# Retention woven into a two-layer network on one core: two of a block's four visits move to the first layer, and sums, casts and waits are placed anew

## The chip, the core and the metric

The kernel runs on 1 core of one Trainium2 chip. The metric is the device time of one launch in microseconds (us), the median of several runs. Before the change it is 301.63 us, with runs between 301.53 and 302.08.

Five engines work side by side, each through its own list of instructions in order: TensorE (PE; its weight loads are shown as PEld), VectorE (DVE), ScalarE (ACT), GpSimd (POOL) and SyncE (SP), which here only issues loads and DMA transposes. An engine waits for another by semaphores.

## The reference

Two parts, one after the other. The first is retention: for each of 8 batches and 8 heads, with 576 positions of 64 numbers, scores are multiplied by a decay that falls with the distance and is zero for later positions. The second is a network of two layers on the 4608 tokens.

```python
gamma = 1.0 - 2.0 ** (-5.0 - np.arange(H))
Dmat = np.where(rel >= 0, gamma[:, None, None] ** rel[None, :, :], 0.0)
attn = np.matmul(scale * np.matmul(q, k.transpose(0, 1, 3, 2)) * Dmat, v)
x = attn.transpose(0, 2, 1, 3).reshape(B * S, H * D)      # 4608 x 512
h = x @ w_in                                              # 4608 x 2048
out = (h * np.cos(h)) @ w_out                             # 4608 x 512
```

## The kernel before

The tokens are worked in nine blocks of 512 (`TB`, block number `j`). Blocks 0 and 1 have a warm-up order of their own; blocks 2 to 8 are one loop (lines 1056 to 1062).

**First layer of a block** (`mlp1`): sixteen groups `dt` of four matmuls 128x512, each into one of four accumulator banks `mm`. ScalarE makes the cosine (`cb`, line 552), VectorE multiplies (`gt`, line 554). Behind each group `steps1` may put a sum, a store, or nothing.

**Second layer** (`mlp2`): the product of 512 tokens x 2048 with 2048 x 512 is cut into halves of tokens, of the contraction and of the columns, and made from seven products of half size instead of eight (`product`, numbers 1 to 7). Each has sixteen matmuls 128x256. For this VectorE makes sums of halves of `gt` (`ssum`, kinds 1 to 4 in four pairs each, tile `ss`, line 576); sums of halves of `w_out` (`ts`) are made once. ScalarE keeps partial results (`keep`, tile `u`), VectorE adds them up (`total`, tile `osb`, line 642).

**Retention** runs in chunks `g` of 128 tokens, 36 in all. One "visit" (`visit`, `quarters`) holds up to 64 small matmuls 64x64 in one woven stretch on TensorE: the outputs of chunk g (in the accumulators `po` and `st`) and the scores and state of chunk g+1 (in `sc`). Behind it ScalarE copies the outputs into `xt`, the input of the first layer, VectorE masks the scores (`rt`, line 753) and adds the running state (`pf`, line 764), and ScalarE casts the state (`sm`, `sn`), the second of the two only at the next visit (`self.old`). Block j visits chunks 4j+4 to 4j+7, whose outputs block j+1 needs. All four visits stand in the second layer, between products: P1 P2 visit P5 visit P6 visit P7 visit P4 P3.

**A chunk's way in**: SP loads k, q and v (`load_g`), GpSimd casts k and scales q and v (`casts_g`, lines 357 to 365), SP transposes k and q by DMA (`turn_dma`, tile `kqt`). `prep(g)` emits the casts and the transposes of chunk g and then calls `pump`, which issues waiting loads of later chunks as long as at most `AHEAD` = 9 load buffers of 16 are taken (three for a chunk). So SP's list is transposes of one chunk, loads of a later one, and so on. In block j, `prep` takes chunks 4j+5 to 4j+8 behind groups 2, 5, 8 and 11. GpSimd is held by nothing but its data and the reuse of the nine slots of a chunk.

`group` makes one list of matmuls with one wait ahead of all of them: a product waits for every sum that it reads before its first matmul.

## Time and profile before

| what | value |
|---|---|
| median of the runs | 301.63 us (301.53 to 302.08) |
| the profiled execution's own time | 301.94 us |
| its span, first to last instruction | 300.2 us |
| mean granted TensorE clock | 0.994 |
| bytes moved by DMA | 49.70 MB |
| read from HBM, written to it | 36.70 MB, 9.44 MB |

The profile is one execution, on one core. "Busy" leaves out waits. In a list of instructions in order of time, a row has its start, the busy time of the merged run, engine, line, operation, tiles as out<-in, shapes and count; in brackets stands the idle time before it and what ended it. "issue" is idle time in which the engine waited for nothing that the profile shows. A window row gives for a stretch the busy time and the count of instructions of each engine, then the granted clock and the DMA's busy share (over 1 where packets of several queues overlap).

### The profile page before, as it was taken

What the parts mean: (1) busy time and instruction counts of PE and PEld (TensorE: products, weight loads), DVE (VectorE), ACT (ScalarE), POOL (GpSimd) and SP (SyncE); (2) the same over time, 40 slices, a digit from 0 to 9 for tenths busy, and PEclk for the clock granted to TensorE, in tenths of its full rate; (3) what the DMA queues carried; (4) which work ended last, traced back from release to release, by engine and by line L of the source; (5) the groups of instructions that cost most, each with busy time, mean ns of one, the idle gap of its engine ahead of it and who ended that gap; (6) DMA issues with size and microseconds to landing.
All of it is one profiled execution on the core that took longest, in us unless ns stands there. A gap on an engine that the chain in (4) does not pass through costs nothing.

```text
span 300.2 us, 8398 instructions
## 1 busy us (share of the span) xinstructions
PE 290.0 (97%) x3532; PEld 181.1 (60%) x3558; DVE 225.4 (75%) x465; ACT 180.7 (60%) x344; POOL 100.1 (33%) x120
## 2 busy tenths in 40 slices
PE   8999999999999999999999979999999999999996
PEld 3474455645454587458745755477547854885485
DVE  3666666766868976998699965979697869766973
ACT  6788435886457645774577435855585567465720
POOL 3670336663634654345436542525000000000000
PEclk9999999999999999999999989999999999999999
DMA  6999999999999999999999999999300130013013
GB/s 206 237 207 192 211 321 194 290 199 179 225 209 251 209 192 186 258 201 172 238 243 232 192 197 238 213 226 161 105 2 2 38 107 0 3 37 107 0 37 105
DMA packets 142325, 49.70 MB, mean 166 GB/s; under 512 B 125904, under 2 KB 141264, under 8 KB 142288
## 3 DMA queue, kind: packets, MB, share of 16 engines
q1 hardware_dynamic: 129280, 35.53, 66.7%
q10 hardware_dynamic: 8784, 9.44, 10.2%
q0 software_dynamic: 4224, 4.19, 8.5%
q8 instruction: 28, 0.46, 0.7%
q14 instruction: 9, 0.07, 0.1%
HBM read 36.70 MB, written 9.44 MB: 154 GB/s over the span
## 4 chain that ended last, share of the span: by engine, by line
PE 88%; DVE 8%; issue 2%; ACT 1%; DVEq 0%
PE mm L461 63%; PE mm L463 15%; DVE gt L554 3%; PE st L708 2%; DVE ss L576 2%; PE sc L708 2%; PE sc L461 2%; PE po L708 1%; PE po L461 1%; DVE rt L485 1%; PE st L461 1%; DVE pf L764 1%; DVE rt L753 0%; ACT cb L552 0%; ACT sb L342 0%
## 5 line engine op out<-in xcount | busy, mean ns | idle before, releaser
L552 ACT ACTIVATE cb<-mm,c_pih 128x512 bf16<-128x512 f32 (+3 forms) x156 | 100.7, 654 | 34.6 <-PE mm L463 34.4
L461 PE MATMUL mm<-xt,win 128*128 128x512 bf16 (+3 forms) x452 | 114.7, 362 | 0.8 <-DVE gt L554 0.3
L554 DVE TENSOR_TENSOR gt<-mm,cb 128x512 bf16<-128x512 f32 (+3 forms) x156 | 99.1, 646 | 20.9 <-ACT cb L552 17.9
L461 PEld LDWEIGHTS mm<-xt,win 128*128 128x128 bf16 x468 | 44.4, 98 | 47.4 <-DVE gt L554 1.3
L463 PE MATMUL mm<-xt,win 128*128 128x512 bf16 (+3 forms) x156 | 56.6, 363 | 0.4
L461 PE MATMUL mm<-wout,gt 128*128 128x256 bf16 (+1 forms) x298 | 49.2, 304 | 1.1 <-issue 0.8
L461 PE MATMUL mm<-ts,ss 128*128 128x256 bf16 x300 | 36.2, 273 | 1.1 <-DVE ss L576 1.0
L365 POOL TENSOR_TENSOR vb<-ld,wv 128x512 bf16<-128x512 f32 x27 | 29.6, 1095 | 22.8 <-DMA ld<-in_v_dram 13.8
L461 PEld LDWEIGHTS mm<-wout,gt 128*128 128x128 bf16 x306 | 28.2, 98 | 13.2 <-DVE gt L554 1.1
L342 POOL CAST kq<-ld 128x512 bf16<-128x512 f32 (+1 forms) x29 | 18.4, 634 | 49.8 <-DMA ld<-in_k_dram 47.9
L361 POOL TENSOR_TENSOR kq<-ld,uq 128x512 bf16<-128x512 f32 x27 | 28.9, 1071 | 14.6 <-DMA ld<-in_q_dram 14.4
L342 ACT ACTIVATE xt<-po 128x256 bf16<-128x256 f32 (+1 forms) x35 | 14.7, 419 | 27.4 <-PE st L708 18.8
L461 PEld LDWEIGHTS mm<-ts,ss 128*128 128x128 bf16 x300 | 27.8, 98 | 5.3 <-DVE ss L576 1.2
L753 DVE TENSOR_TENSOR rt<-sc,mh 128x256 bf16<-128x256 f32 x54 | 20.3, 417 | 12.9 <-PE st L708 9.7
L576 DVE TENSOR_TENSOR ss<-gt 128x512 bf16<-128x512 bf16 x56 | 26.9, 480 | 0.2
L642 DVE TENSOR_TENSOR osb<-mm,u 128x512 f32<-128x512 f32 x20 | 13.8, 688 | 17.3 <-PE mm L463 14.6
L463 PEld LDWEIGHTS mm<-xt,win 128*128 128x128 bf16 x156 | 15.2, 98 | 16.0
L342 ACT ACTIVATE u<-mm 128x512 f32<-128x512 f32 x21 | 12.5, 597 | 19.4 <-PE mm L463 19.3
L764 DVE TENSOR_TENSOR pf<-sc,pf 128x256 f32<-128x256 f32 x42 | 17.6, 420 | 2.0
L342 ACT ACTIVATE sm<-pf 128x256 bf16<-128x256 f32 x24 | 10.0, 417 | 10.6 <-DVE pf L764 8.7
L463 PE MATMUL mm<-wout,gt 128*128 128x512 bf16 (+1 forms) x46 | 15.9, 347 | 0.1
L461 PE MATMUL mm<-ts,gt 128*128 128x256 bf16 x105 | 13.9, 289 | 0.1
(154 smaller groups left out, 370.9 us busy)
## 6 DMA issues: line engine op xcount, KB each, us to landing
out_dram<-osb ACTq DMA_DIRECT2D x35, 256.0 KB, 4.3
ld<-in_k_dram SPq DMA_DIRECT2D x32, 256.0 KB, 4.9
ld<-in_q_dram SPq DMA_DIRECT2D x32, 256.0 KB, 4.8
ld<-in_v_dram SPq DMA_DIRECT2D x32, 256.0 KB, 6.2
win<-in_moe_w_in_dram POOLq DMA_DIRECT2D x4, 512.0 KB, 8.3
wout<-in_moe_w_out_dram POOLq DMA_DIRECT2D x4, 512.0 KB, 15.1
ld<-in_k_dram SPq DMA_DIRECT2D x8, 128.0 KB, 4.3
ld<-in_q_dram SPq DMA_DIRECT2D x8, 128.0 KB, 4.0
```

The lines of the kernel that those rows point to most:

```text
L342: fn = (lambda e: e.activation(o, x, AF.Copy)) if eng == "act" else (lambda e: e.tensor_copy(o, x))
L361: self.s.op("pool", lambda e: e.tensor_tensor(o, a, w, ALU.mult), reads=[bt, self.bUQ], writes=[self.bQB[i]])
L365: self.s.op("pool", lambda e: e.tensor_tensor(o2, a2, w2, ALU.mult), reads=[bt, self.bWV], writes=[self.bVB[i]])
L461: self.nc.tensor.matmul(o, a, b, **kw)
L463: return s.done("pe", self.nc.tensor.matmul(o, a, b, **kw), reads, writes)
L552: s.op("act", lambda e: e.activation(ci, mi, AF.Sin, bias=self.C_PIH.ap(), scale=1.0), reads=[bm, self.bC], writes=[self.bCB[i]])
L554: s.op("dve", lambda e: e.tensor_tensor(bass.AP(self.GT, dt * TB + o0, [[16 * TB, 128], [1, n]]), mi, ci, ALU.mult), reads=[bm, self.bCB[i ...
L576: self.s.op("dve", lambda e: e.tensor_tensor(self.s_(k, d), a, b, op), reads=rd, writes=[S[k - 1][p]])
L642: self.s.op("dve", lambda e: e.tensor_tensor(o, m, x, ALU.add), reads=[bm, self.bU[u]], writes=[self.bOSB[i]])
L708: inst = self.nc.tensor.matmul(o, a, c, **kw)
L753: s.op("dve", lambda e: e.tensor_tensor(bass.AP(self.RT[n % 2][x], 0, p3), bass.AP(self.SC[x], 0, p3), bass.AP(self.MH, 0, [[64, 128], [0, ...
L764: s.op("dve", lambda e: e.tensor_tensor(self.PF[t].ap(), u, self.PF[1 - t].ap(), ALU.add), reads=[self.bSU[t], self.bPF[1 - t]], writes=[s ...
```

## The change

- **Visits**: in block j the first two visits come in the first layer, behind groups 4 and 10; the third stands behind P2, the fourth behind P7. The order of the second layer is P1 P2 visit P6 P5 P7 visit P4 P3.
- **What follows a visit** (masks, copies into `xt`, adds, casts) is put on a list (`todo`) and emitted from it by `flush`: two entries behind each first-layer group, six or all at set places of the second layer, the rest ahead of the next visit.
- **Sums**: in the first layer only two pairs of kind 1 are left, behind group 14; all others stand in the second layer, in runs of four to six. (The last block has kind 3 in the first layer, behind groups 8 to 11.)
- **Products wait by pairs**: a product is four groups of four matmuls, each with a wait for its own pair of sums.
- **GpSimd** waits, behind group 0 of a first layer, for that group's last matmul (`need`), and `prep` takes chunks 4j+7 to 4j+10 behind groups 0, 3, 6 and 9; chunks 13 and 14 are taken during block 1's second layer.
- **Loads**: from chunk 16 on, up to 12 load buffers may be taken.

```diff
@@ product
-        self.group(mms, ra + rb, bms)
+        for p in range(4):
+            self.group([(bass.AP(ms[tt], tt * HN, [[512, 128], [1, HN]]), a(d, tt), b(d),
+                         dict(...)) for d in (2 * p, 2 * p + 1) for tt in tts],
+                       ra(p) + rb(p), bms)
@@ quarters
+        halves = [t for t in range(2) if n is not None and n % 9 != (4, 8)[t]]
+        for x in range(2):
+            self.todo += [(mask, x) if n is not None else None, (xt, x) if g is not None else None]
+        self.todo += [(add, t) if t in halves else None for t in range(2)] + [None, None]
+        for t in halves:
+            self.todo += [(cast, t), None]
+
+    def flush(self, n=None):
+        for _ in range(len(self.todo) if n is None else min(n, len(self.todo))):
+            u = self.todo.pop(0)
+            if u:
+                u[0](u[1])
@@ mlp2
         br = self.take()
         self.product(br, 2, True, True)
-        self.ssum(2, 0)
-        self.ssum(2, 1)
-        vis(0)
...
+        self.ssum(1, 2)
+        self.ssum(1, 3)
+        for p in range(4):
+            self.ssum(2, p)
+        for g in visits[:1]:
+            self.visit(g)
+        self.flush(6)
         self.product(bs, 6, False, False)
         self.keep(bs, 1)
+        self.flush()
+        i11 = self.total(br, 0)
+        if not last:
+            for p in range(4):
+                self.ssum(3, p)
+        bt = [(self.SC[t], self.bSC[t]) for t in range(2)] if last else self.take()
+        self.product(bt, 5, True, False)
         self.store(i11, j, 0, 0)
+        for p in range(4):
+            self.ssum(4, p)
         self.product(bs, 7, False, last)
         self.keep(bs, 2)
...
+        for g in visits[1:]:
+            self.visit(g)
+        self.flush(6)
@@ steps1
-        if dt in (2, 4, 6, 8):
-            self.ssum(3, dt // 2 - 1)
-        if dt in (10, 12, 14):
-            self.ssum(1, dt // 2 - 5)
+        if dt == 14:
+            self.ssum(1, 0)
+            self.ssum(1, 1)
+        if j == NTB - 1 and dt in (8, 9, 10, 11):
+            self.ssum(3, dt - 8)
@@ pump
-                if fn == self.load_g and sum(self.busy) + n > AHEAD:
+                if fn == self.load_g and sum(self.busy) + n > (AHEAD if a[0] < 4 * 4 else AHEAD + 3):
@@ emit
             if n in (1, 5, 9, 13):
                 self.visit(G0 + n // 4 - 1)
-            elif T and n:
+                self.flush()
+            if n in (6, 10):
+                self.prep(G0 + 3 + n // 5)
+            if T and n not in (0, 1, 5, 9, 13):
                 self.tsum("dve", *T.pop(0))
...
         for j in range(2, NTB):
+            g = 4 * j + 4 if j < NTB - 1 else NG
             for dt in range(16):
                 self.mlp1(j, dt)
+                self.flush(2)
                 self.steps1(j, dt)
-                if dt % 3 == 2 and dt < 12:
-                    self.prep(4 * j + 5 + dt // 3)
-            self.mlp2(j, range(4 * j + 4, 4 * j + 8) if j < NTB - 1 else [])
+                if dt == 0:
+                    self.s.need("pool", [self.last])
+                if dt % 3 == 0 and dt < 12:
+                    self.prep(g + 3 + dt // 3)
+                if dt in (4, 10) and g < NG:
+                    self.visit(g + dt // 6)
+            self.mlp2(j, range(g + 2, min(g + 4, NG)))
```

More of the change, by code (lines that the diff above doesn't have):

```diff
@@ L233, in __init__ @@
         self.order = [0, 1, 2, 3]
-        self.old = None
+        self.todo = []
     def build(self):
@@ L547, in mlp1 @@
                 dict(start=c == 0, stop=c == 3)) for c in range(4)]
-        self.group(mms, [self.bWIN[dt // 4]] + self.bXT[t0 // GR:(t0 + n) // GR], [bm])
+        self.last = self.group(mms, [self.bWIN[dt // 4]] + self.bXT[t0 // GR:(t0 + n) // GR], [bm])
         i = self.n_cb % self.NCB
@@ L602, in ga @@
             return (lambda d, tt: bass.AP(self.GT, (8 * kh + d) * TB + th * HT + 128 * tt, [[16 * TB, 128], [1, 128]]),
-                    self.bGT[8 * kh:8 * kh + 8])
+                    lambda p: self.bGT[8 * kh + 2 * p:8 * kh + 2 * p + 2])
         def sa(i):
             return (lambda d, tt: bass.AP(self.SS, ((i - 1) * 8 + d) * HT + 128 * tt, [[32 * HT, 128], [1, 128]]),
-                    self.bSS[i - 1])
+                    lambda p: [self.bSS[i - 1][p]])
         def wb(kh, nh):
             return (lambda d: bass.AP(self.WOUT, (8 * kh + d) * DM + nh * HN, [[16 * DM, 128], [1, HN]]),
-                    self.bWOUT[8 * kh:8 * kh + 8])
+                    lambda p: self.bWOUT[8 * kh + 2 * p:8 * kh + 2 * p + 2])
         def tb(i):
-            return (lambda d: bass.AP(self.TS, ((i - 1) * 8 + d) * HN, [[32 * HN, 128], [1, HN]]), [self.bTS[i - 1]])
+            return lambda d: bass.AP(self.TS, ((i - 1) * 8 + d) * HN, [[32 * HN, 128], [1, HN]]), lambda p: [self.bTS[i - 1]]
         (a, ra), (b, rb) = {1: (ga(0, 0), wb(0, 0)), 2: (ga(0, 1), wb(1, 0)), 3: (sa(4), wb(1, 1)),
                             4: (ga(1, 1), tb(4)), 5: (sa(1), tb(1)), 6: (sa(2), tb(2)), 7: (sa(3), tb(3))}[k]
-        mms = [(bass.AP(ms[tt], tt * HN, [[512, 128], [1, HN]]), a(d, tt), b(d),
-                dict(start=start and d == 0 and (tt == tts[0] or ms[0] is not ms[1]), stop=stop and d == 7, skip_group_check=True))
-               for d in range(8) for tt in tts]
-        self.group(mms, ra + rb, bms)
+        for p in range(4):
+            self.group([(bass.AP(ms[tt], tt * HN, [[512, 128], [1, HN]]), a(d, tt), b(d),
+                         dict(start=start and d == 0 and (tt == tts[0] or ms[0] is not ms[1]), stop=stop and d == 7,
+                              skip_group_check=True)) for d in (2 * p, 2 * p + 1) for tt in tts],
+                       ra(p) + rb(p), bms)
     def osb(self):
@@ L735, in quarters @@
                             [self.bQT[i]] + [self.bSM if t else self.bSN[(g - 1) % 2] for t in ts], [bXY[x]], None)]
-        if self.old:
-            sn, t, bsn = self.old
-            self.copy("act", sn.ap(), self.PF[t].ap(), [self.bPF[t]], [bsn])
-            self.old = None
-        self.weave(*[cross[x] + score[x] + state[x] + own[x] + past[x] for x in range(2)])
-        if g is not None:
-            x0 = CH * g % XR
-            w = self.bXT[x0 // GR:(x0 + CH) // GR]
-            for x in range(2):
-                t = self.copy("act", bass.AP(self.XT, 2 * x * XR + x0, [[NP * XR, 128], [XR, 2], [1, CH]]),
-                              bass.AP(self.XY[x], 0, [[512, 128], [CH, 2], [1, CH]]), [bXY[x]], [Buf()] if x else w)
-            for u in w:
-                u.w.append(t)
@@ L749, in quarters @@
-        if n is not None:
-            m = n % 9
-            for x in range(2):
-                p3 = [[512, 128], [64, NP], [1, 64]]
-                s.op("dve", lambda e: e.tensor_tensor(
-                    bass.AP(self.RT[n % 2][x], 0, p3), bass.AP(self.SC[x], 0, p3),
-                    bass.AP(self.MH, 0, [[64, 128], [0, NP], [1, 64]]), ALU.mult),
-                    reads=[self.bSC[x], self.bSU[x], self.bMH], writes=[self.bRT[n % 2][x]])
-            for t, sn, bsn in ((0, self.SM, self.bSM), (1, self.SN[n % 2], self.bSN[n % 2])):
-                if m == (4, 8)[t]:
-                    continue
-                u = bass.AP(self.SC[t], 256, [[512, 128], [1, NP * D_]])
-                if m == 4 * t:
-                    self.copy("dve", self.PF[t].ap(), u, [self.bSU[t]], [self.bPF[t]])
-                else:
-                    s.op("dve", lambda e: e.tensor_tensor(self.PF[t].ap(), u, self.PF[1 - t].ap(), ALU.add),
-                         reads=[self.bSU[t], self.bPF[1 - t]], writes=[self.bPF[t]])
-                if t:
-                    self.old = (sn, t, bsn)
-                else:
-                    self.copy("act", sn.ap(), self.PF[t].ap(), [self.bPF[t]], [bsn])
@@ L771, in mlp2, with xt @@
-    def mlp2(self, j, visits):
-        s = self.s
-        v = list(visits) + [None] * 4
-        def vis(n):
-            if v[n] is not None:
-                self.visit(v[n])
+        self.flush()
+        self.weave(*[cross[x] + score[x] + state[x] + own[x] + past[x] for x in range(2)])
+        x0 = CH * g % XR if g is not None else 0
+        w = self.bXT[x0 // GR:(x0 + CH) // GR]
+        def xt(x):
+            t = self.copy("act", bass.AP(self.XT, 2 * x * XR + x0, [[NP * XR, 128], [XR, 2], [1, CH]]),
+                          bass.AP(self.XY[x], 0, [[512, 128], [CH, 2], [1, CH]]), [bXY[x]], [Buf()] if x else w)
+            for u in w if x else ():
+                u.w.append(t)
@@ new lines, in mask, with add @@
+        def mask(x):
+            p3 = [[512, 128], [64, NP], [1, 64]]
+            s.op("dve", lambda e: e.tensor_tensor(
+                bass.AP(self.RT[n % 2][x], 0, p3), bass.AP(self.SC[x], 0, p3),
+                bass.AP(self.MH, 0, [[64, 128], [0, NP], [1, 64]]), ALU.mult),
+                reads=[self.bSC[x], self.bSU[x], self.bMH], writes=[self.bRT[n % 2][x]])
+        def add(t):
+            u = bass.AP(self.SC[t], 256, [[512, 128], [1, NP * D_]])
+            if n % 9 == 4 * t:
+                self.copy("dve", self.PF[t].ap(), u, [self.bSU[t]], [self.bPF[t]])
+            else:
+                s.op("dve", lambda e: e.tensor_tensor(self.PF[t].ap(), u, self.PF[1 - t].ap(), ALU.add),
+                     reads=[self.bSU[t], self.bPF[1 - t]], writes=[self.bPF[t]])
@@ new lines, in cast @@
+        def cast(t):
+            sn, bsn = (self.SN[n % 2], self.bSN[n % 2]) if t else (self.SM, self.bSM)
+            self.copy("act", sn.ap(), self.PF[t].ap(), [self.bPF[t]], [bsn])
+        halves = [t for t in range(2) if n is not None and n % 9 != (4, 8)[t]]
[4 more added lines that the diff above has]
+            self.todo += [(cast, t), None]
@@ L780, in mlp2 @@
+    def flush(self, n=None):
[3 more added lines that the diff above has]
+                u[0](u[1])
+    def mlp2(self, j, visits):
         last = j == NTB - 1
-        self.ssum(1, 3)
         bs = self.take()
@@ L786, in mlp2 @@
         self.product(br, 2, True, True)
-        self.ssum(2, 0)
-        self.ssum(2, 1)
-        vis(0)
-        bt = [(self.SC[t], self.bSC[t]) for t in range(2)] if last else self.take()
-        if not last:
-            self.product(bt, 5, True, False)
-        self.ssum(2, 2)
-        self.ssum(2, 3)
-        i11 = self.total(br, 0)
-        vis(1)
+        self.ssum(1, 2)
[5 more added lines that the diff above has]
+        self.flush(6)
         self.product(bs, 6, False, False)
         self.keep(bs, 1)
-        self.store(i11, j, 0, 0)
-        self.ssum(4, 0)
-        self.ssum(4, 1)
-        vis(2)
-        if last:
-            self.product(bt, 5, True, False)
+        self.flush()
[5 more added lines that the diff above has]
+        self.product(bt, 5, True, False)
+        self.store(i11, j, 0, 0)
+        for p in range(4):
+            self.ssum(4, p)
         self.product(bs, 7, False, last)
         self.keep(bs, 2)
-        self.ssum(4, 2)
-        self.ssum(4, 3)
         i22 = self.osb()
@@ L811, in mlp2 @@
             self.total(bt, 2, i22, t, 1 if last else 2)
-        vis(3)
+        for g in visits[1:]:
+            self.visit(g)
+        self.flush(6)
         if not last:
@@ L1051, in emit @@
                 self.visit(G0 + n // 4 - 1)
-            elif T and n:
+                self.flush()
+            if n in (6, 10):
+                self.prep(G0 + 3 + n // 5)
+            if T and n not in (0, 1, 5, 9, 13):
                 self.tsum("dve", *T.pop(0))
```

## The prediction

> **What bounds the kernel now.** The page first: which engine is busy, whether the DMA is full, and how the code itself is fetched.

> ```profile
> span 300.2 us, 8398 instructions
> PE 290.0 (97%) x3532; PEld 181.1 (60%) x3558; DVE 225.4 (75%) x465; ACT 180.7 (60%) x344; POOL 100.1 (33%) x120
> ...
> DMA  6999999999999999999999999999300130013013
> ...
> q8 instruction: 28, 0.46, 0.7%
> ...
> PE 88%; DVE 8%; issue 2%; ACT 1%; DVEq 0%
> ```

> TensorE holds 88% of the chain that ended last. So only two things can shorten the run: less TensorE work, which the change does not bring (its matmuls are the same in number and shape), or the removal of its stalls. The DMA is full for the first 28 slices of 7.5 us, about 210 us. The row of the instruction queue counts 28 packets; TensorE has 3532 + 3558 = 7090 instructions, 253 for each packet, so this queue brings TensorE's own code, a page of some 253 instructions at a time.

> Second view: one window for each of the blocks 2 to 7 of 512 tokens, from its first matmul to the next block's. Columns: us, then busy time (and instructions) of each engine, granted clock, DMA share, GB/s.

> ```profile
> 89.12:118.88 29.76, 29.66 (x416) 19.59 (x417) 24.58 (x52) 19.04 (x36) 15.15 (x16) 1.00 1.29 209
> 118.88:148.71 29.83, 29.62 (x414) 19.42 (x416) 25.21 (x50) 18.33 (x35) 13.00 (x15) 1.00 1.18 215
> 148.71:182.35 33.64, 31.39 (x414) 20.34 (x416) 26.87 (x50) 18.38 (x35) 16.48 (x18) 0.95 1.23 214
> 182.35:212.46 30.11, 29.37 (x414) 19.50 (x416) 25.07 (x50) 18.45 (x35) 12.59 (x14) 1.00 1.08 206
> 212.46:241.97 29.51, 29.36 (x414) 19.52 (x416) 23.20 (x50) 18.26 (x35) 0.00 (x0) 1.00 0.11 38
> 241.97:271.44 29.47, 29.24 (x390) 19.27 (x392) 21.85 (x46) 18.20 (x34) 0.00 (x0) 1.00 0.12 38
> ```

> Blocks 6 and 7, where GpSimd (fifth busy column) is done and the DMA nearly idle, take 29.5 us. Blocks 2 to 5 do the same matmuls beside casts and a full DMA and take more. Six quiet blocks would be 6 x 29.47 = 176.82 us against 182.32 now: **5.50 us of stalls**, 4.17 of them in block 4. The third view is TensorE's order of time there.

> ```profile
> 171.70 0.22 PE L708 MATMUL st<-rt,vb 64*64 64x64 bf16 x2
> ...
> 174.91 0.19 PE L708 MATMUL po<-kqt,sm 64*64 64x64 bf16 x1
> 176.82 0.21 PE L708 MATMUL po<-kqt,sm 64*64 64x64 bf16 x1 [1.72 <-issue]
> ...
> 173.96:177.37 3.41, 1.70 (x72) 1.29 (x71) 3.31 (x8) 1.21 (x4) 2.09 (x2) 1.00 1.27 167
> 177.37:180.78 3.41, 3.41 (x18) 2.37 (x17) 0.24 (x1) 1.12 (x4) 0.81 (x2) 0.50 1.08 219
> ...
> 169.85 0.28 PE L461 MATMUL mm<-ts,ss 128*128 128x256 bf16 x1 [0.39 <-DVE ss L576]
> ...
> 203.52 0.28 PE L461 MATMUL mm<-ts,ss 128*128 128x256 bf16 x1 [0.59 <-DVE ss L576]
> ```

> TensorE stops for 1.72 us inside a group of retention matmuls that waits for nothing ("issue"): I read it as code that has not come. A stretch ("visit") has up to 64 load-and-matmul pairs, 128 instructions, and a product 16 pairs, 32; from 171.70 to 174.91 a visit, a product and nearly another visit, some 260 instructions, run in 3.2 us, so a whole page is used up while the next is fetched through full DMA engines. Right after it the granted clock is 0.50 for 3.41 us, which costs 1.70 more. The windows of 3.41 us have the columns of the second view; the last two rows are waits for VectorE's sums, 0.39 and 0.59.

> **The change part by part.** *The fetch stall.* Two of a block's four visits go to the first layer, behind its groups 4 and 10; the other two stay in the second. Between two visits there now lie at least three products (P6, P5, P7) or six first-layer groups.

> ```profile
> 89.12 0.81 PE L461 MATMUL mm<-xt,win 128*128 128x512 bf16 x3
> ...
> 102.94 1.80 PE L461 MATMUL mm<-wout,gt 128*128 128x256 bf16 x15
> ...
> 104.68 1.81 PE L461 MATMUL mm<-wout,gt 128*128 128x256 bf16 x15
> ...
> 106.53 0.22 PE L708 MATMUL st<-rt,vb 64*64 64x64 bf16 x2
> ...
> 107.33 1.81 PE L461 MATMUL mm<-ts,ss 128*128 128x256 bf16 x15
> ```

> Sixteen first-layer groups take 13.82 us, 0.864 each; a product 1.74; a visit 0.80. A page of 253 instructions that holds three products (96) and 157 of visits lasts 5.2 + 157/128 x 0.80 = 6.2 us, twice the 3.2 that stalled. So the stall goes: -1.72, and with it the half clock, -1.70. [...]

> *Sums in second layers, casts held to first ones.* GpSimd now waits, at each block's start, for the first group of the first layer; behind this wait stand the casts of four chunks, behind these SP's transposes, behind these the next loads.

> ```profile
> L576 DVE TENSOR_TENSOR ss<-ss,gt x16: 411/418/1266, 105.1 to 202.2; 128x512 bf16<-128x512 bf16 x16
> ...
> L576 DVE TENSOR_TENSOR ss<-ss,gt x8: 415/418/419, 228.1 to 261.7; 128x512 bf16<-128x512 bf16 x8
> ...
> L365 POOL TENSOR_TENSOR vb<-ld,wv 128x512 bf16<-128x512 f32 x27 | 29.6, 1095 | 22.8 <-DMA ld<-in_v_dram 13.8
> L342 POOL CAST kq<-ld 128x512 bf16<-128x512 f32 (+1 forms) x29 | 18.4, 634 | 49.8 <-DMA ld<-in_k_dram 47.9
> L361 POOL TENSOR_TENSOR kq<-ld,uq 128x512 bf16<-128x512 f32 x27 | 28.9, 1071 | 14.6 <-DMA ld<-in_q_dram 14.4
> ```

> A sum takes 0.42 us in the quiet blocks and up to 1.27 beside casts (minimum, median, maximum in ns). Four chunks are 4 x (1.10 + 0.63 + 1.07) = 11.2 us of casts, inside the 15.5 us that the first layer has with two visits. The two waits for sums go, -0.98. What is left of the 5.50, 1.10 us in small excesses of blocks 2 to 5, has the same neighbours; between 0 and -1.10 I take -0.80. The held casts cost nothing while their cover stands: a block's first transposes are needed only by the third visit, 13.8 + 1.6 + 3.5 = 19 us after its start, and loads for four chunks at the 6.7 us of a chunk (84.92 to 91.64 below) fit 29.5 us by 3. Without that cover a block would wait up to the 6.7 us of one chunk.

> *VectorE and ScalarE in the first layer.*

> ```profile
> 120.59 0.69 ACT L552 ACTIVATE cb<-mm,c_pih 128x512 bf16<-128x512 f32 x1 [0.18 <-PE mm L463]
> ...
> 121.31 0.69 DVE L554 TENSOR_TENSOR gt<-mm,cb 128x512 bf16<-128x512 f32 x1 [0.17 <-ACT cb L552]
> ...
> 123.58 1.27 DVE L554 TENSOR_TENSOR gt<-mm,cb 128x512 bf16<-128x512 f32 x2
> ...
> 107.01 0.76 DVE L753 TENSOR_TENSOR rt<-sc,mh 128x256 bf16<-128x256 f32 x2 [1.14 <-PE sc L708]
> ...
> 110.51 0.94 DVE L764 TENSOR_TENSOR pf<-sc,pf 128x256 f32<-128x256 f32 x2
> ```

> A product (gt) back to back takes a slot of 0.60; the masks of a visit are 0.7, its two adds 0.9. First layer: 16 x 0.60 + 2 x 1.6 + 2 sums 0.7 = 13.5 of 15.5 us, so VectorE fits. The latest lag follows the two adds, about 0.75 us. A group's bank is wanted again four groups, 3.45 us, after the group began; the cosine starts some 1.05 us after that beginning and gt ends 121.31 + 0.69 - 120.59 = 1.41 us later, so about 0.95 is spare. No stall; if slots did not overlap, 1.15 - 0.95 = 0.2 and 0.45 at the second layer's second product: 0.65 a block is the upper bound, 0 my value. Seven products split in four groups each add boundaries, whose waits are mostly met by then: each first-layer group waits too, and 0.864 is four times 0.216. I cost them at 0, as I do the gaps at a visit's edges, which move but keep their number.

> *Loads ahead of transposes.* From chunk 16 on one more chunk is in flight: SP now issues the three loads of chunk 16 ahead of chunk 13's transposes (the first transposes below; the loads of 16 are the three at 88.41 to 89.66).

> ```profile
> 84.92 3.45 SPq L390 DMA_TRANSPOSE kqt<-kq  x1
> 88.41 0.58 SPq L317 DMA_DIRECT2D ld<-in_k_dram  x1
> 89.03 0.58 SPq L317 DMA_DIRECT2D ld<-in_q_dram  x1
> 89.66 1.86 SPq L317 DMA_DIRECT2D ld<-in_v_dram  x1
> 91.64 2.70 SPq L390 DMA_TRANSPOSE kqt<-kq  x1
> ...
> DMA to landing us min/median/max: 4.4/5.6/7.1
> ```

> The three loads take 3.2 us, so these transposes go out at 88.1 and land at 92.5 to 95.2 (median 93.7). And they are wanted earlier: the scores of chunk 13 ran in the visit of 106.53, now they run behind group 4 of block 2, 89.12 + 5 x 0.864 + 0.1 = 93.5. **A new wait of 0 to 1.7 us** in block 2; I take 0.9, nearer to the middle than to the median's 0.2, since these transposes took 7.1 in the old order. Chunk 14 is wanted 6 us later and lands about 5.5 later; from there on the margin grows.

> Sum: -3.42 - 0.98 - 0.80 + 0.90 = **-4.3 us**. The profiled execution took 301.94 (span 300.2); the median of the runs, 301.63, is 0.31 lower. 301.63 - 4.3 = **297.3**.

> **The rivals.** *B, the late transposes also drop the clock.* At 1.7 us the wait leaves half of a 3.41 us stretch busy, as in the row at 173.96, and the next stretch runs at half clock: 297.3 + 0.8 + 1.7 = 299.8. For it: that row. Against: 0.59 of idle time at 203.52 dropped nothing, so the point lies between. [...]

> *C, the stall is not one of visit density and comes back*: + 3.42, 300.7. For it: the other visit-product-visit series did not stop. Against: where a page ends decides that.

> *D, slower: VectorE sets the second layer.* Six sums now stand in one series behind the last gt, and P6's first pair needs the third of them: gt ends about 2.7 us into the second layer, three sums of 0.36 make 3.8, P6 starts at 4.4. If GpSimd still casts then, three sums at +0.85 make 2.55 - 0.6 = 1.9 us of stall; in four blocks with casts 7.7: 305. It decides once loads land later than some 14 us into a block. Against: 11.2 of 15.5 us.

> *E, the change does not do what it says*, stalls only move: 301.6.

> **How the numbers follow.** Forecast 0.62 (295.6 to 299), B 0.13, C 0.10, D 0.10, E 0.05. Range: low without the new wait and with the whole 1.10, 301.63 - 5.5 - 0.5 for the bounded gaps = 295.6; high just past C, 300.8, leaving out D, E and some of C. A run tells 0.2%, 0.6 us, from no change: faster is the forecast, B and most of C, 0.82; same 0.08; slower 0.10.

> **What would show it.** Right: no issue idle time over 1 us behind block 2, granted clock 1.00 throughout, blocks 3 to 7 at 29.4 to 29.6 us, sums near 0.42, casts ending before each first layer does, and block 2 longer by a wait for kqt near 93.5. Wrong: TensorE waiting for ss in several second layers, for gt in first ones, or a clock of 0.50 anywhere.

## The result, and the profile after

The changed kernel takes **297.8 us** (median of 7 runs, 296.87 to 299.12) against 301.53 for the kernel before (7 runs, 299.66 to 304.17): ratio 0.9895, 95% interval 0.9859 to 0.993. A second set on another occasion (label r1_changed) gave 298.25 against 302.2, ratio 0.9864 (0.9825 to 0.9904). The forecast was 297.3. Ratios leave out runs more than 1.5% above the fastest of their kernel, medians take all, so the two do not divide exactly.

The first rows of the page after; the DMA row has 40 equal slices, the last row is the chain by engine.

```profile
span 297.4 us, 8336 instructions
...
PE 285.3 (96%) x3526; PEld 180.6 (61%) x3558; DVE 214.6 (72%) x465; ACT 173.9 (58%) x344; POOL 95.6 (32%) x120
...
DMA  6999999999999999999999965899591170013013
...
PE 84%; DMA 9%; issue 2%; SPq 2%; DVE 1%; ACT 1%; DVEq 0%
```

The DMA is now full for 23 slices and then works in bursts; before, it was full for 28. VectorE's share of the chain fell from 8% to 1%, and DMAs now have 9%: loads of the opening, and the transposes (`kqt`) of one chunk in block 2. The windows of blocks 2 to 7, with the columns of the windows before:

```profile
90.76:121.67 30.91, 29.29 (x416) 19.69 (x417) 23.05 (x52) 17.64 (x35) 10.57 (x12) 1.00 1.19 203
121.67:151.00 29.33, 28.96 (x413) 19.56 (x416) 22.99 (x50) 17.21 (x35) 10.30 (x12) 1.00 1.21 218
151.00:180.41 29.41, 29.04 (x413) 19.59 (x416) 22.91 (x50) 17.22 (x35) 10.29 (x12) 1.00 0.96 195
180.41:209.84 29.43, 29.02 (x414) 19.55 (x416) 22.91 (x50) 17.21 (x35) 10.29 (x12) 1.00 0.93 180
209.84:239.34 29.50, 29.09 (x414) 19.57 (x416) 22.81 (x50) 17.21 (x35) 10.30 (x12) 1.00 0.53 100
239.34:268.77 29.43, 28.94 (x390) 19.39 (x393) 21.40 (x46) 17.21 (x35) 2.62 (x3) 1.00 0.21 47
```

Blocks 3 to 7 all take 29.3 to 29.5 us, what only the quiet blocks took before, at a clock of 1.00 throughout. Block 2 has grown to 30.91. The six blocks sum to 178.01 us, 4.31 less than the 182.32 of before. The span shrank by only 2.8 because the opening, up to the first matmul of block 2, was 1.64 us longer in this one execution (90.76 against 89.12). The opening moves that much between profiles of kernels that share it: r6, below, has 89.16.

What block 2 waits for, in TensorE's order of time (start, us, instruction, and in brackets the idle time before it and what ended it):

```profile
95.23 0.20 PE L709 MATMUL po<-rt,vb 64*64 64x64 bf16 x2
96.68 0.32 PE L709 MATMUL sc<-kqt 64*64 64x64 bf16 x16 [1.25 <-DMA kqt<-kq]
```

And the order of time of SP's DMA queue ahead of it:

```profile
84.49 0.94 SPq L317 DMA_DIRECT2D ld<-in_v_dram  x1
85.47 1.76 SPq L317 DMA_DIRECT2D ld<-in_k_dram  x1
87.27 1.14 SPq L317 DMA_DIRECT2D ld<-in_q_dram  x1
88.45 2.61 SPq L317 DMA_DIRECT2D ld<-in_v_dram  x1
91.10 2.84 SPq L390 DMA_TRANSPOSE kqt<-kq  x1
```

The scores of chunk 13 wait 1.25 us for its transposes, which SP could issue at 91.10 only, behind the three loads of chunk 16 (issued from 85.47 to 88.45). One of the three rows of the sums of blocks 2 to 7 (minimum, median, maximum in ns; the longest of the other two is 421):

```profile
L576 DVE TENSOR_TENSOR ss<-ss,gt x24: 418/419/420, 110.8 to 258.9; 128x512 bf16<-128x512 bf16 x24
```

No sum is longer than 0.42 us where 1.27 occurred. The first and the last cast of block 3, in GpSimd's order of time:

```profile
122.55 0.61 POOL L342 CAST kq<-ld 128x512 bf16<-128x512 f32 x1 [15.28 <-PE mm L463]
...
131.80 1.05 POOL L365 TENSOR_TENSOR vb<-ld,wv 128x512 bf16<-128x512 f32 x1
```

GpSimd stands for 15.28 us, until block 3's first group is done, and then casts four chunks in 10.3 us, well inside the first layer. The hold does not empty the DMA in the second layers, though. The one of block 3 as a window:

```profile
135.35:150.68 15.33, 15.33 (x241) 12.70 (x239) 13.05 (x34) 7.05 (x16) 0.00 (x0) 1.00 1.19 201
```

TensorE is busy for 15.33 of 15.33 us beside a full DMA (1.19). In the same windows of blocks 2 and 5 the share is 1.14 and 1.11.

### The profile page after: what moved, and what is told of

It is laid out like the page before. It is cut to its first block, busy times and chain, and to the rows that moved or that the text cites. A ratio compares the mean times of both kernels' runs of the same rounds, so it can differ in the third digit from the quotient of the medians.

```text
span 297.4 us, 8336 instructions
## 1 busy us (share of the span) xinstructions
PE 285.3 (96%) x3526; PEld 180.6 (61%) x3558; DVE 214.6 (72%) x465; ACT 173.9 (58%) x344; POOL 95.6 (32%) x120
## 4 chain that ended last, share of the span: by engine, by line
PE 84%; DMA 9%; issue 2%; SPq 2%; DVE 1%; ACT 1%; DVEq 0%
PE mm L461 56%; PE mm L463 19%; DMA ld<-in_q_dram 3%; PE st L709 3%; PE sc L709 2%; DMA win<-in_moe_w_in_dram 2%; DMA ld<-in_v_dram 2%; DMA kqt<-kq 2%; SPq L290 2%; PE po L709 2%; PE sc L461 1%; PE po L461 1%; PE st L461 0%; PE sc L463 0%; ACT cb L552 0%
## 5 line engine op out<-in xcount | busy, mean ns | idle before, releaser
L554 DVE TENSOR_TENSOR gt<-mm,cb 128x512 bf16<-128x512 f32 (+3 forms) x156 | 99.4, 647 | 35.0 <-ACT cb L552 34.0
L552 ACT ACTIVATE cb<-mm,c_pih 128x512 bf16<-128x512 f32 (+3 forms) x156 | 100.7, 654 | 37.3 <-PE mm L463 36.4
L461 PE MATMUL mm<-xt,win 128*128 128x512 bf16 (+3 forms) x446 | 113.4, 362 | 3.1 <-issue 1.9
L461 PEld LDWEIGHTS mm<-xt,win 128*128 128x128 bf16 x468 | 43.5, 98 | 45.2 <-DVE gt L554 0.8
L463 PE MATMUL mm<-xt,win 128*128 128x512 bf16 (+3 forms) x156 | 56.6, 363 | 0.1
L342 POOL CAST kq<-ld 128x512 bf16<-128x512 f32 (+1 forms) x29 | 17.7, 610 | 117.4 <-PE mm L463 100.6
L461 PE MATMUL mm<-wout,gt 128*128 128x256 bf16 (+1 forms) x256 | 49.1, 309 | 1.0 <-issue 0.8
L461 PE MATMUL mm<-ts,ss 128*128 128x256 bf16 x240 | 35.4, 273 | 0.0
L461 PEld LDWEIGHTS mm<-wout,gt 128*128 128x128 bf16 x264 | 24.7, 98 | 11.8 <-DVE gt L554 0.5
L342 ACT ACTIVATE u<-mm 128x512 f32<-128x512 f32 x21 | 12.5, 597 | 32.3 <-PE mm L463 32.3
L365 POOL TENSOR_TENSOR vb<-ld,wv 128x512 bf16<-128x512 f32 x27 | 28.4, 1052 | 6.4 <-DMA ld<-in_v_dram 4.0
L361 POOL TENSOR_TENSOR kq<-ld,uq 128x512 bf16<-128x512 f32 x27 | 28.2, 1044 | 4.3 <-DMA ld<-in_q_dram 4.3
L342 ACT ACTIVATE xt<-po 128x256 bf16<-128x256 f32 (+1 forms) x35 | 14.6, 418 | 23.0 <-PE st L709 15.7
L463 PE MATMUL mm<-wout,gt 128*128 128x256 bf16 (+1 forms) x88 | 27.4, 311 | 0.1
L643 DVE TENSOR_TENSOR osb<-mm,u 128x512 f32<-128x512 f32 x20 | 13.8, 688 | 18.8 <-PE mm L463 11.2
L750 DVE TENSOR_TENSOR rt<-sc,mh 128x256 bf16<-128x256 f32 x54 | 21.2, 416 | 5.9 <-PE st L709 2.5
L463 PEld LDWEIGHTS mm<-xt,win 128*128 128x128 bf16 x156 | 15.3, 98 | 16.0
L461 PEld LDWEIGHTS mm<-ts,ss 128*128 128x128 bf16 x240 | 23.0, 98 | 2.8
L463 PE MATMUL mm<-ts,ss 128*128 128x256 bf16 x80 | 21.8, 272 | 0.0
L576 DVE TENSOR_TENSOR ss<-gt 128x512 bf16<-128x512 bf16 x56 | 20.7, 417 | 0.0
L709 PE MATMUL po<-rt,vb 64*64 64x64 bf16 x216 | 13.4, 202 | 0.1
```

The lines of the kernel that those rows point to most:

```text
L342: fn = (lambda e: e.activation(o, x, AF.Copy)) if eng == "act" else (lambda e: e.tensor_copy(o, x))
L361: self.s.op("pool", lambda e: e.tensor_tensor(o, a, w, ALU.mult), reads=[bt, self.bUQ], writes=[self.bQB[i]])
L365: self.s.op("pool", lambda e: e.tensor_tensor(o2, a2, w2, ALU.mult), reads=[bt, self.bWV], writes=[self.bVB[i]])
L461: self.nc.tensor.matmul(o, a, b, **kw)
L463: return s.done("pe", self.nc.tensor.matmul(o, a, b, **kw), reads, writes)
L552: s.op("act", lambda e: e.activation(ci, mi, AF.Sin, bias=self.C_PIH.ap(), scale=1.0), reads=[bm, self.bC], writes=[self.bCB[i]])
```

## The experiments

Each kernel was run beside the kernel before on one chip. "Ratio" is against the kernel before, with its 95% interval; where kernels shared a chip, medians are compared directly.

### r1_changed, r2_visits_back, r3_no_hold, r4_loads9

r1 is the changed kernel itself. r2 puts all visits back into the second layer:

```diff
-                if dt in (4, 10) and g < NG:
-                    self.visit(g + dt // 6)
-            self.mlp2(j, range(g + 2, min(g + 4, NG)))
+            self.mlp2(j, range(g, min(g + 4, NG)))
@@ mlp2
+        for g in visits[1:2]:
+            self.visit(g)
+        self.flush(6)
         self.product(bt, 5, True, False)
...
+        for g in visits[2:3]:
+            self.visit(g)
+        self.flush(6)
         self.product(bs, 7, False, last)
```

r3 takes GpSimd's hold away, r4 the fourth chunk in flight:

```diff
-                if dt == 0:
-                    self.s.need("pool", [self.last])
@@ pump
-                ... sum(self.busy) + n > (AHEAD if a[0] < 4 * 4 else AHEAD + 3):
+                ... sum(self.busy) + n > AHEAD:
```

> The changed kernel again, beside the variants on one chip. My theory: the four stalls of before are gone and one new wait of about 1.25 us for chunk 13's transposes is in block 2; time 297 to 298 us, blocks 3 to 7 at 29.3 to 29.5 us each, clock 1.00 throughout. Rival (the fetch stall comes back in some runs): a profile with an issue wait over 1 us behind block 2, and runs spread by 3 us.

> All four visits back in the second layer (behind P2, P6, total and P7), all else as changed. Fetch theory: visit, product, visit, product again uses up a page of code in about 3 us, so issue waits of 1 to 2 us come back in some blocks with a full DMA, some with a half clock behind them, 1 to 4 us slower than the changed kernel; the first new wait (chunk 13) goes, 1.2 us, since the visits come later. Rival (density does not matter, the sums were the cost): no issue wait, 1 us faster than the changed kernel by the chunk 13 wait.

> GpSimd not held to first layers. Contention theory: casts run beside the second layers' sums again, sums of up to 1.27 us, and TensorE waits for ss between 0.3 and 1.9 us in each of blocks 3 to 5: 1 to 5 us slower than the changed kernel. Rival (the hold is worth nothing since the sums have room): sums up to 1.27 us, but no wait of TensorE, time within 0.5 us.

> At most 9 load buffers throughout, so chunk 13's transposes go out ahead of chunk 16's loads. My theory: the 1.25 us wait for kqt in block 2 goes or shrinks below 0.3, 296 to 296.5 us, 1.0 to 1.3 us faster than the changed kernel, if later loads still come in time. Rival (the fourth chunk in flight is needed): the last chunk of a block's loads is late, GpSimd's casts run past the first layer, and sums or visits wait in blocks 3 to 5; same time or slower.

| kernel | median us | ratio |
|---|---|---|
| before (20 runs) | 302.2 | |
| r1, changed | 298.25 | 0.9864 (0.9825 to 0.9904) |
| r2, visits back | 303.18 | 1.0048 (1.0015 to 1.008) |
| r3, no hold | 305.13 | 1.0093 (1.0062 to 1.0125) |
| r4, 9 load buffers | 296.89 | 0.982 (0.9781 to 0.9859) |

r1 came 0.25 us above the 297 to 298 that were expected; its wait for chunk 13 was 1.7 us in its profile.

r2 is slower, but for neither reason that was named. One of TensorE's waits, in order of time:

```profile
140.38 0.22 PE L709 MATMUL po<-kqt,sn 64*64 64x64 bf16 x2 [0.43 <-ACT sm L342]
```

From the list of its waits (total us, number, longest), and ScalarE ahead of that wait:

```profile
PE po L709 <- ACT sm L342: 3.2, 8, 0.5
PE mm L461 <- issue: 0.8, 5, 0.2
...
139.42 0.60 ACT L342 ACTIVATE u<-mm 128x512 f32<-128x512 f32 x1 [1.11 <-PE mm L463]
139.91 0.41 ACT L342 ACTIVATE sm<-pf 128x256 bf16<-128x256 f32 x1
```

No issue wait exceeds 0.4 us in four crowded visits a block, although the DMA is full in the second layers of blocks 2 and 3 (shares 1.21 and 1.12). Why this profile has no fetch stall there is not shown; one of the twelve runs, of 305.81 us, has a mean clock of 0.994. What costs time is the state cast `sm`, which a visit needs: it stands in ScalarE's list behind the `keep` (`u`) of the product just ahead of that visit, and ScalarE idles 1.11 us until that product ends. That is some 0.4 to 0.5 us once or twice a block, with further small gaps; blocks 2 to 7 take 30.1 to 30.6 us. The test is confounded: it shows that four visits do not fit this order of the second layer, not what the move does by itself.

r3 decides for contention, and harder than expected: 6.9 us above r1. TensorE, VectorE and GpSimd in block 3's second layer, in order of time:

```profile
143.28 0.50 PE L461 MATMUL mm<-wout,gt 128*128 128x256 bf16 x3 [1.18 <-DVE gt L554]
...
141.36 1.26 DVE L576 TENSOR_TENSOR ss<-gt 128x512 bf16<-128x512 bf16 x1
...
141.12 1.22 POOL L365 TENSOR_TENSOR vb<-ld,wv 128x512 bf16<-128x512 f32 x1
```

A sum that begins beside a scaling of v lasts 1.26 us, ends 0.28 us behind it, and delays the last gt, for which the second product waits 1.18. This is the contention of the prediction's rival D, once the hold is gone. Of the scaling 0.98 us were left when the sum began, and the sum lasted 0.84 longer than the 0.42 of a sum alone; by what the one holds up the other the trace does not show. r3 has the visits spread out but no hold, and a full DMA in the second layers of blocks 2 and 3; its profile has no issue wait over 0.2 us.

r4 settles the new wait: without the three loads ahead the wait for kqt is gone from the list of TensorE's waits, and the kernel is 1.36 us faster than r1. All that comes instead is one wait of 0.30 us for gt in block 2.

### r5_before_again, r6_dense_code, r7_before_hold, r8_whole_waits

r5 is the kernel before, for a second profile. r6 adds a run of code to the changed kernel (extra matmuls on a zero tile, their results not used; one run, 320.08 us); r7 is the kernel before with the hold alone; r8 the changed kernel with one wait for each whole product.

```diff
@@ r6
                 self.mlp1(j, dt)
+                if dt == 8 and j in (3, 8):
+                    self.dense(384)
...
+    def dense(self, n):
+        m, bm = self.MM[self.order[0]], self.bMM[self.order[0]]
+        self.group([(bass.AP(m, 64 * (i % 2) * 512, [[512, 64], [1, 64]]),
+                     bass.AP(self.IDLE, 64 * (i % 2) * 512, [[512, 64], [1, 64]]),
+                     bass.AP(self.IDLE, 64 * (i % 2) * 512, [[512, 64], [1, 64]]),
+                     dict(start=True, stop=True, skip_group_check=True)) for i in range(n)], [self.bIDLE], [bm])
@@ r7
+                if dt == 0:
+                    self.s.need("pool", [self.last])
@@ r8
-        for p in range(4):
-            self.group([... for d in (2 * p, 2 * p + 1) for tt in tts], ra(p) + rb(p), bms)
+        self.group([... for d in range(8) for tt in tts],
+                   sum([ra(p) + rb(p) for p in range(4)], []), bms)
```

> Another profile of the kernel before. Fetch theory with chance in it: an issue wait of 1 to 2 us inside a visit again, perhaps at another place, since the fetch through a full DMA is late by chance; blocks 2 to 5 together 2 to 6 us above four quiet ones (29.5 each). Rival (the stall in the first profile was a rare event and the usual cost of before is VectorE): no issue wait over 1 us, and waits for ss instead.

> 384 extra pairs of small matmuls (768 instructions, about three pages of code, on a zero tile, results unused) behind group 8 in blocks 3 and 8 of the changed kernel. At the pace of a visit they take some 4 us. Fetch theory: in block 3, with the DMA full, they are held up by issue waits of 1 to 2 us a page, 3 to 6 us in all; in block 8, with the DMA nearly idle, clearly less, 0 to 3 us. Rival (fetches do not limit): both runs take 4 us without an issue wait.

> The kernel before with the hold of GpSimd alone. Contention theory: sums of the second layers fall to 0.42 us and TensorE's waits for ss go (0.98 us in the first profile) with part of the small excesses; the fetch stalls stay: 0.5 to 2 us faster than before. Rival (the hold needs the new places of sums and visits): casts now meet the seven sums of the first layer, gt is late, and the time is the same or up to 2 us slower.

> The changed kernel with one wait for a whole product instead of four. My theory: the second product waits for the last gt and the product P6 for all four sums of kind 2, which end about 0.1 to 0.3 us after it could start: 0.2 to 0.5 us a block, 1 to 3 us in all, slower than the changed kernel. Rival (the pairs are worth nothing): within 0.5 us.

r5 (one run, 304.03 us) stalls at the same place of the program, the last visit of block 4, for 2.22 us, and the clock is 0.50 from 178.25 to 181.66. Its blocks 2 to 5 are 7.2 us above four quiet ones, more than the 2 to 6 expected. TensorE in order of time:

```profile
176.01 0.19 PE L708 MATMUL po<-kqt,sm 64*64 64x64 bf16 x1
178.42 0.26 PE L708 MATMUL po<-kqt,sm 64*64 64x64 bf16 x1 [2.22 <-issue]
```

The two stretches of 3.41 us by windows:

```profile
174.84:178.25 3.41, 1.36 (x67) 1.01 (x65) 3.25 (x8) 1.18 (x3) 1.66 (x2) 1.00 1.38 219
178.25:181.66 3.41, 3.24 (x18) 2.32 (x19) 0.19 (x1) 0.96 (x3) 1.04 (x1) 0.50 0.71 155
```

The half clock is the exception. Of 82 runs of the kernel before that stood beside the variants, 18 have a mean clock of 0.993 or 0.994, which is what one half-speed stretch of 3.41 us leaves; the other 64 have 0.999 or 1.000. Their medians are 303.9 and 301.8 us. Both profiled executions of this kernel, the first one and r5 (0.994 each), are of the rarer kind.

r6 shows the fetch itself. The extra matmuls, in block 3 with the DMA full (share 1.03) and in block 8 with it nearly idle (0.02):

```profile
129.00 3.35 PE L461 MATMUL mm<-idle 64*64 64x64 bf16 x199
134.37 2.21 PE L461 MATMUL mm<-idle 64*64 64x64 bf16 x128 [2.03 <-issue]
139.20 1.07 PE L461 MATMUL mm<-idle 64*64 64x64 bf16 x56 [2.61 <-issue]
...
288.27 3.95 PE L461 MATMUL mm<-idle 64*64 64x64 bf16 x237
293.43 2.21 PE L461 MATMUL mm<-idle 64*64 64x64 bf16 x128 [1.21 <-issue]
296.89 0.47 PE L461 MATMUL mm<-idle 64*64 64x64 bf16 x18 [1.24 <-issue]
```

Between two waits lie exactly 128 matmuls with their 128 loads, in block 3 and in block 8: a page of code is 256 instructions here. It runs in 2.2 us, but TensorE begins the next only 139.20 - 134.37 = 4.83 us after it began this one, and with the nearly idle DMA 296.89 - 293.43 = 3.46. The full DMA goes with 1.4 us more, on one interval each.

The packets of the instruction queue, 16384 bytes each, tell that the stalls of the kernel before are the same thing. The one ahead of its stall ends at 175.48, and TensorE goes on 1.34 us later, at 176.82; in r5 it is 1.25 us, in the four waits of r6 1.4 to 1.6. The waits for sums in the same trace have no such distance (0.33 and 3.08).

r7: the hold alone gives 301.32 against 302.54 (22 runs), ratio 0.9979 (0.9954 to 1.0004), at best a small gain. None of its 12 runs has the clock of 0.994, against 6 of the 22 beside it. The second layer of block 4 by windows, in the kernel before:

```profile
162.39:182.03 19.64, 17.50 (x353) 13.93 (x351) 14.44 (x30) 8.07 (x20) 9.41 (x11) 0.91 1.28 197
```

The same in r7:

```profile
163.50:179.74 16.24, 15.92 (x353) 13.23 (x352) 11.99 (x31) 8.17 (x20) 0.00 (x0) 1.00 0.76 153
```

A wait of TensorE in r7:

```profile
135.28 1.81 PE L461 MATMUL mm<-wout,gt 128*128 128x256 bf16 x15 [0.28 <-DVE gt L554]
```

With the hold no cast runs in the second layer (0 instructions of GpSimd against 11), the DMA share falls from 1.28 to 0.76, and the stall with its half clock is not there, although the visits are as crowded as before: SP's next transposes wait for casts (one is issued in this window, against four before), and the loads behind them wait too. That the stalls would stay, as was expected, was wrong. What takes the gain back is the last gt of each block, late by the casts in the first layer (the longest sum of r7 takes 1.06 us), for which the second product waits as a whole, 0.28 us a block, with other small gaps; one of these, 0.41 us in the last but one visit of block 3, comes up again with r10.

r8: 304.61 us, ratio 1.0086 (1.0052 to 1.0119), 6.4 us above the changed kernel's 298.25 of the other chip session. That is twice the upper end of what was expected, and the expected wait of P6 for sums shows only as 0.2 us in the whole run. A wait of TensorE in block 3:

```profile
140.80 1.81 PE L461 MATMUL mm<-wout,gt 128*128 128x256 bf16 x15 [0.82 <-DVE gt L554]
```

All of its kind (total us, number, longest):

```profile
PE mm L461 <- DVE gt L554: 4.5, 8, 0.8
```

A whole wait puts the second product up to 0.82 us later, behind the last gt, which two sums have delayed. These waits are 4.2 us more than in r1; the rest of the 6.4 was not taken apart.

### r9_before_shift, r10_before_hold_pairs, r11_loads9_again, r12_before_pairs

r9 is the kernel before with `self.dense(20)` behind its first ten warm-up matmuls (results not used): 40 instructions, so each page of code ends 40 instructions earlier in the same work. r10 is r7 with the changed kernel's `product`, so hold and pairs, but visits and sums at their old places. r11 is r4 again. r12 is r10 without the hold.

> The kernel before with 20 extra pairs of small matmuls (40 instructions, on a zero tile, results unused) in TensorE's opening, where it waits for the first data: the same work in the same order, but every page of code ends 40 instructions earlier in it. By the times of the first profile no page of blocks 2 to 5 is then used up in less than 4.1 us (3.0 where it stalled). Fetch theory: the stall of block 4 and its half clock go, 2.5 to 3.5 us faster than before, 298.7 to 299.7. Rival (the stall belongs to the place, a visit beside a burst of transposes): it stays, same time as before, and a clock of 0.50 in block 4.

> The kernel before with the hold of GpSimd and waits by pairs, but visits and sums at their old places. Theory (pairs cure the late gt that the hold alone brought, 0.28 us a block; what is left to the visits' move is the fetch stall): 299 to 300.5 us, blocks 2 to 6 at 29.5 to 30, sums of the second layer 0.42 us. Rival (the new places of sums and visits carry the gain): 301 us and more, with waits for gt or ss left.

> The changed kernel with 9 load buffers throughout, again, beside the two others: 296.5 to 297.3 us, below both of them and below the changed kernel's 298.

> The kernel before with waits by pairs alone, GpSimd free. Theory (the hold takes the full DMA and the casts out of the second layers, and so both the fetch stalls and the long sums; pairs only shorten waits that are there): the DMA share of the second layers of blocks 2 to 5 stays at 1.0 to 1.4, an issue wait over 1 us comes back in block 4, 300.5 to 302 us, 0 to 1.3 us faster than before. Rival (pairs alone carry the gain of the hold with pairs): 298 to 299 us and no issue wait.

| kernel | median us | before beside it | ratio |
|---|---|---|---|
| r9, pages shifted | 301.35 | 301.83 | 1.0003 (0.9968 to 1.0037) |
| r10, hold and pairs | 298.3 | 301.83 | 0.9909 (0.988 to 0.9938) |
| r11, changed with 9 buffers | 296.95 | 301.83 | 0.9865 (0.9816 to 0.9914) |
| r12, pairs alone | 301.26 | 302.42 | 0.9946 (0.9905 to 0.9986) |

r9 missed its number, 2.5 to 3.5 us: the median is 0.5 us lower, the ratio 1.0003, so no gain is shown. None of its 12 runs has the clock of 0.994, against 5 of the 23 beside it. In its profile the stall of block 4 is 1.16 us without a half clock, but others stand where there were none:

```profile
147.97 0.60 PE L461 MATMUL mm<-ts,gt 128*128 128x256 bf16 x4 [0.86 <-issue]
...
177.29 0.21 PE L715 MATMUL po<-rt,vb 64*64 64x64 bf16 x1 [1.16 <-issue]
```

Each of these ends 1.4 us behind a packet of the instruction queue, too. Moving nothing but the ends of pages moved the stalls, as the fetch theory says; it did not remove them. That many pages of the crowded second layers are used up in less than the 4.83 us of r6 would fit, but was not counted. Reckoning single page ends from a trace was too fine.

r12: without the hold the fetch stall is back, in block 3 this time. The wait in order of time:

```profile
143.33 0.22 PE L709 MATMUL po<-rt,vb 64*64 64x64 bf16 x2 [1.72 <-issue]
```

That second layer by windows:

```profile
132.27:149.59 17.32, 15.60 (x352) 13.27 (x351) 13.88 (x30) 8.10 (x21) 8.38 (x9) 1.00 1.18 220
```

Its runs spread from 298.88 to 306.03, and 5 of 12 have the clock of 0.994; those of r10 spread from 297.53 to 299.32, and none has it. Of the two, the kernel with the longer stall in its profile has the more uneven times. The theory held, the place was another. r10, the same program with the hold, stops at the very same place of its code:

```profile
143.00 0.22 PE L709 MATMUL po<-rt,vb 64*64 64x64 bf16 x2 [0.68 <-PE sc L709]
```

The profile puts this wait down to TensorE's own scores, but it ends 1.26 us behind a packet of the instruction queue, like the stalls above (r12: 1.58). So in these two profiles the stall is 0.68 us with the hold and 1.72 without, with the DMA share of that second layer at 0.97 instead of 1.18; the hold did not abolish it. The 0.41 us in r7 stand at the same place and end 1.38 us behind a packet.

r10 is the surprise. Hold and pairs alone give 298.3 us, as much as the whole change within the intervals. Beside it, r11 is 1.35 us faster: that is what the new places of visits and sums add when the loads do not go ahead of the transposes, and the loads (r1 against r4, 1.36 us) take just that back. r11 and r4 are the fastest version tried, about 1.4 us below the changed kernel.

## Why the prediction was right

**The sum.** Forecast -4.3; the six blocks lost 4.31 us in the profiles, the medians 3.7 and 3.95. The range and the direction held. The terms did less well than their sum, and that the blocks agree to 0.01 us is luck.

**Fetch stall and half clock, -3.42.** Right that they go: no issue wait over 0.2 us behind block 2, and a clock of 0.999 or 1.000 in all 13 runs. The mechanism is borne out: the waits lie between pages of code (128 matmuls and 128 loads in r6) and end 1.25 to 1.6 us behind a packet of the instruction queue. The step from spacing to no stall held as well: in the second layers of blocks 2, 3 and 5 the DMA is as full (1.11 to 1.19) as where r12 stalled (1.18), and no issue wait stands there. That is not proof, since r2's profile has none with crowded visits beside a full DMA either. What the prediction did not see is a second remedy: with the visits left crowded, the hold goes with a less full DMA (share 1.18 to 0.97, r12 to r10) and a shorter stall (1.72 to 0.68). The half of the term that is the clock, -1.70, was luck in the sum. It was taken from one execution and off the median of the runs, but 64 of 82 runs of the kernel before have no half clock, and the median lies among them. What they lose in its place was not profiled; the nearest, r9's execution of 301.6 us without a half clock, loses 5.1 us in blocks 2 to 5 by issue waits of 0.56, 0.86 and 1.16 and by waits for gt and sums. Rival C fell: the stall did not come back in either profile of the changed kernel, nor the half clock in any of its runs.

**The hold, -1.78 in all with the small excesses.** Right in kind, too small in what depends on it. Priced as two waits and some excess, its removal from the changed kernel costs 6.9 us (r3): the new series of sums lives from it, as rival D had it. That D's time, 305, is met by 305.13 is partly luck: D had 1.9 us in each of four blocks, and against the changed kernel they lost 2.5, 3.1, 1.5 and 0.6.

**Waits by pairs, 0.** Mis-sized. I priced the added boundaries, which show no cost, and not the cover that they give: without them the changed kernel is 6.4 us slower (r8), and on the hold they bring 301.32 to 298.3 across two sessions (r7 to r10).

**VectorE in the first layer, 0.** Right: blocks 3 to 7 are at 29.3 to 29.5 us, and no gt is waited for there.

**The late transposes, +0.9 between 0 and 1.7.** Right in place and cause, too small in size: 1.25 and 1.7 us in two profiles, the upper part of the range; r4 removes it for 1.36. Rival B did not come: neither wait halved the clock (mean 1.000 in both profiles).

## What to carry to other kernels

When an engine needs much code in little time beside a full DMA, look for issue waits inside groups that wait for nothing, count instructions for each page of code, and ask what else fills the DMA just then. With two remedies the stalls were shorter here: spreading the small matmuls (r3, no issue wait over 0.2 us in its profile), and a wait on an idle-looking engine that thinned the DMA in the crowded stretch (r12 to r10, share 1.18 to 0.97, stall 1.72 to 0.68 us). Ask in how many runs a profiled stall occurs before it is taken off their median. Price a split of waits by what it lets the producer be late, not by its boundaries. And read the issuing queue whenever a buffer limit is raised: three loads let in early stood ahead of the one transfer that was due, for a wait of 1.25 us.

## What the runs showed of the hardware that I had not expected

TensorE went on 1.25 to 1.6 us after a packet of the instruction queue had ended, in each of the fetch stalls above for which the distance is given.

With idle time of 1.72 us (the kernel before), 2.22 (r5) and 2.61 (r6) came 3.41 us at half the clock (0.50, in r6 from 140.21 to 143.62); with 1.25 and 1.7 in the changed kernel and 2.03 in r6 none came. Nor did one with 1.72 us in r12, with TensorE busy for 1.69 of the 3.41 us, as good as the 1.70 before the half clock of the first profile:

```profile
141.38:144.79 3.41, 1.69 (x55) 1.45 (x40) 3.31 (x8) 1.67 (x5) 1.06 (x3) 1.00 1.18 260
144.79:148.21 3.42, 3.42 (x90) 2.91 (x88) 1.89 (x6) 1.77 (x5) 1.98 (x2) 1.00 1.05 177
```

That a stretch half busy halves the clock, as rival B had it, these records do not show: 1.70 us of busy time stood ahead of half the clock, 1.69 did not, and the idle time was 1.72 us both times. What decides it stays open.
